# A new instruction order for a cross-attention and PReLU kernel, with a third buffer for its exponentials

## The chip, the cores and the metric

The kernel runs on one core of one Trainium2 chip. The metric is the device time of one execution in microseconds (us). The profile's *span*, from the first to the last instruction, is about 1.75 us shorter than that time. Engines: PE (TensorE, matmuls), ACT (ScalarE), DVE (VectorE), POOL (GpSimd), and SP, which here only issues DMAs. PSUM, where PE writes, has eight banks.

## What is computed

There are 8 batches, 8 heads, 512 tokens, 32 states, 64 features a head. Tokens attend to states, states attend to tokens, both results are put behind each other as 544 rows a batch of 512 features, and these go through a two-layer network with a PReLU.

```python
scores = scale * np.matmul(x, state.transpose(0, 1, 3, 2))
a = softmax(scores);   xread = np.matmul(a, state)        # 512 rows a batch
scores2 = scale * np.matmul(state, x.transpose(0, 1, 3, 2))
a2 = softmax(scores2); sread = np.matmul(a2, x)           # 32 rows a batch
x = concatenate([xread, sread], axis=2)                   # as rows of 8 * 64 features
h = x @ w_in                                              # 512 -> 2048
g = np.maximum(h, 0.0) + alpha * np.minimum(h, 0.0)
out = g @ w_out                                           # 2048 -> 512
```

## The kernel before

Since `xread @ w_in` is `a @ (state @ w_in)`, the kernel first makes the small state product m = state @ w_in, and the token weights a then meet m directly. All work is cut into steps, and the string `ORDER` (lines 17 to 102) lists them by hand, 1053 tokens. The loop at its end calls the steps in that order under a manual schedule, so each engine works through its own share of the list in exactly this order, and waits where an operand or a buffer isn't ready. A token names a step and its arguments; the last numbers of m, F, S, rd are PSUM banks k0 to k5, the last letter of mo, O, rdo the engine that copies (a is ACT, v is DVE). The steps that matter here, for batch b:

- `sc.b` (PE): both score products into the two-bank PSUM tile `two`, whose single buffer also serves some products m. It needs `xd.b`, a DMA that transposes x, issued by SP, which in turn needs `lx.b`, the load of x, issued by POOL.
- `tm.b`, `sb.b`, `smax.b` (DVE): the maximum over states, the scores' block transpose, the maximum over tokens. `te.b.g` (ACT): exponentials for the state reads, into the tile `e2`. `ssh`, `snorm` (POOL), `sexp` (ACT), `ssum`, `wb` (DVE): the rest of the token softmax, which ends in the weights aT.
- `tn.b.g` (POOL) scales `e2`; `tt.b` (SP) transposes it by DMA; `rd.b` (PE) are the state reads, `rdo.b` their copy.
- `m.b.f` (PE): a quarter f of the state product. Without banks in the token it goes to the two-bank tile (`m.0.3`, `m.1.3`, `m.6.0` and others), with banks (`m.5.1.2.0`) to two single ones. `mo.b.f.e.g` copies half g of it to SBUF on engine e. Its eight matmuls run in parallel on parts of the array, so one m takes about as long as one and a half matmuls of 512 columns.
- `F.b.jc.k` (PE): two matmuls of 512 columns, 128 hidden features of the batch, into bank k. `N.b.jc` (ACT): relu(-h) out of that bank, into one of four buffers. `G.b.jc` (DVE): the PReLU out of the same bank. After G the bank is free. `F.8.jc` is the same for all batches' state reads at once.
- `S.b.q.i` (PE): two matmuls of 512 columns, the part of hidden features 2i and 2i + 1 of the 128 tokens q; at i = 0 the token names the bank. After i = 7, `O.b.q.e` copies the bank out on engine e and SP writes it to memory (in two DMAs for batch 2, else in one), through four buffers in turn.

In the profile F is line 491 (`f`, its halves, line 512; of the reads line 500), S line 543, N line 523, G line 531, m line 458, mo line 480, sc line 308, rd line 433, O line 581, te line 400, tt line 418, xd line 275, tm line 389 and 392, sb line 341, smax line 349.

The excerpt of the list that the prediction speaks of (m.0.3, m.1.3 with their copies; the softmax of batch 1):

```
te.1.1 te.1.0 F.0.11.3 G.0.9 ssh.p.1 F.0.8.1 N.0.8 N.0.11 S.0.0.3 S.0.1.3 m.0.3 G.0.8 F.0.10.2
mo.0.3.a.0 N.0.10 sexp.1 S.0.2.3 mo.0.3.v.1 xd.2 G.0.11 G.0.10 S.0.3.0.1 m.1.3 S.0.3.1 mo.1.3.a.0
```

Of the kernel before, what the change touches and what calls it, by code (L numbers as in the profile page):

```python
# [38 lines left out]
S.1.1.3 ssum.2 F.1.14.0 F.1.15.2 snorm.p.2 mo.2.3.a.0 S.1.1.4 mo.2.3.a.1 S.1.1.5 m.3.2 m.4.2.1.4
N.1.14 tt.1 tsum.2 N.1.15 G.1.14 mo.3.2.a.1 S.1.1.6 S.1.2.3 S.1.2.4 mo.3.2.a.0 mo.4.2.a.0 G.1.15  # L40
mo.4.2.a.1 S.1.2.5 S.1.1.7 xd.3 O.1.1.a m.3.1.0.2 m.2.2.1.4 sc.3 wb.2 tn.2.1 S.1.2.6 S.1.2.7
mo.3.1.a.1 F.2.15.5 S.1.0.0.2 mo.2.2.a.0 mo.3.1.a.0 O.1.2.a lx.4 mo.2.2.a.1 sb.3 N.2.15 S.1.0.1 tm.3
F.2.13.1 N.2.13 G.2.15 S.1.0.2 F.2.4.0 tn.2.0 F.2.2.3 G.2.13 smax.3 N.2.4 F.2.9.4 F.2.0.5 N.2.9
S.1.0.3 S.1.0.4 G.2.9 S.1.0.5 N.2.2 N.2.0 te.3.0 F.2.12.1 S.1.0.6 N.2.12 G.2.2 G.2.4 G.2.0 xd.4
# [12 lines left out]
S.3.3.0.4 F.3.15.0 S.3.3.1 N.3.5 lx.6 G.3.5 te.5.0 te.5.1 N.3.10 N.3.15 S.2.2.3 F.3.12.5 S.2.2.4
N.3.11 S.3.3.2 lx.7 N.3.12 G.3.10 G.3.15 F.4.6.3 N.4.6 tn.4.0 F.4.5.0 G.3.11 F.4.3.1 N.4.5 S.2.2.5
G.3.12 G.4.5 S.3.3.3 F.4.4.5 S.3.3.4 F.4.7.0 N.4.4 S.3.3.5 S.2.2.6 N.4.3 sb.5 N.4.7 S.3.3.6 S.2.2.7
G.4.4 G.4.7 S.3.3.7 F.4.1.5 F.4.0.0 xd.6 O.2.2.a S.3.1.0.2 O.3.3.a S.3.1.1 F.4.9.4 N.4.1 smax.5  # L60
G.4.6 N.4.0 S.3.0.0.3 tn.4.1 S.3.0.1 G.4.1 G.4.0 F.4.8.5 S.3.1.2 tsum.5 N.4.9 ssh.p.5 G.4.3 sexp.5
N.4.8 G.4.9 F.4.11.0 F.4.2.1 N.4.2 S.3.0.2 ssum.5 S.3.0.3 S.3.0.4 tt.4 N.4.11 S.3.1.3 G.4.8 S.3.1.4
# [590 lines left out]
```

## Time and profile before

| | |
|---|---|
| time, median of 3 runs | 218.55 us (218.24 to 218.85) |
| the profiled execution | 218.35 us, its span 216.6 us |
| granted clock of TensorE | 1.00 throughout |
| matmuls | 1637, of them 746 of 512 columns in F (250) and S (496) |
| DMA | 23.12 MB, mean 107 GB/s |

A line of the profile's groups or of its timeline names the source line, the engine, the operation and what is written from what, with shapes; xN is the number of instructions taken together. In the timeline the first two numbers are start and length in us, and brackets hold the idle time of the engine before it and what ended that. Line 480, for instance, is every copy of a state product, whichever engine makes it. PE's busy time counts from a matmul's start to its modelled end, and matmuls overlap, so how full PE is shows better in the distance from one start to the next.

### The profile page before, as it was taken

What the parts mean: (1) busy time and instruction counts of PE and PEld (TensorE: products, weight loads), DVE (VectorE), ACT (ScalarE), POOL (GpSimd) and SP (SyncE); (2) the same over time, 40 slices, a digit from 0 to 9 for tenths busy, and PEclk for the clock granted to TensorE, in tenths of its full rate; (3) what the DMA queues carried; (4) which work ended last, traced back from release to release, by engine and by line L of the source; (5) the groups of instructions that cost most, each with busy time, mean ns of one, the idle gap of its engine ahead of it and who ended that gap; (6) DMA issues with size and microseconds to landing.
All of it is one profiled execution on the core that took longest, in us unless ns stands there. A gap on an engine that the chain in (4) does not pass through costs nothing.

```text
span 216.6 us, 4193 instructions
## 1 busy us (share of the span) xinstructions
PE 209.9 (97%) x1637; PEld 99.9 (46%) x1637; DVE 166.5 (77%) x253; ACT 137.2 (63%) x271; POOL 71.1 (33%) x58
## 2 busy tenths in 40 slices
PE   7889999999999999999999999999999999999994
PEld 2543334444444444544444445444454455554553
DVE  3699998899899999798998769977798466665001
ACT  3399984899987848786747937566545346544021
POOL 7383943730943703190337301802500000000000
PEclk9999999999999999999999999999999999999999
DMA  6999999496286694179652811041430011110124
GB/s 89 174 196 206 207 199 183 127 206 127 59 137 145 81 213 98 51 108 195 174 109 97 100 50 49 2 97 48 53 147 24 28 48 48 48 47 4 48 100 145
DMA packets 39716, 23.12 MB, mean 107 GB/s; under 512 B 22144, under 2 KB 35984, under 8 KB 39696
## 3 DMA queue, kind: packets, MB, share of 16 engines
q0 software_dynamic: 12704, 8.62, 28.2%
q1 hardware_dynamic: 26960, 14.23, 26.3%
q8 instruction: 13, 0.21, 0.5%
q14 instruction: 7, 0.06, 0.1%
q10 hardware_dynamic: 32, 0.01, 0.0%
HBM read 17.31 MB, written 8.91 MB: 121 GB/s over the span
## 4 chain that ended last, share of the span: by engine, by line
PE 90%; DMA 5%; POOL 2%; issue 1%; DVE 1%; ACT 0%; POOLq 0%
PE o L543 50%; PE h L491 25%; DMA w_in_sb<-in_moe_w_in_dram 5%; PE m_ps L458 4%; PE h L500 3%; PE o L591 3%; PE o L563 2%; PE sr_ps L433 2%; PE sc L308 1%; DVE m L480 1%; POOL xg L179 1%; POOL xg L162 0%; PE h L512 0%; POOL w_in_sb L198 0%; ACT m L480 0%
## 5 line engine op out<-in xcount | busy, mean ns | idle before, releaser
L543 PE MATMUL o<-w_out_sb,gt 128*128 128x512 f16 x496 | 125.3, 379 | 0.0
L523 ACT ACTIVATE neg<-h 128x512 f32<-128x512 f32 (+1 forms) x144 | 77.1, 579 | 46.8 <-PE h L491 37.4
L531 DVE SCALAR_TENSOR_TENSOR gt<-neg,oma_sb,h 128x512 f16<-128x512 f32 x128 | 89.9, 738 | 15.5 <-ACT neg L523 14.5
L543 PEld LDWEIGHTS <-gt 128*128 128x128 f16 x496 | 47.3, 98 | 55.3 <-issue 3.4
L491 PE MATMUL h<-aT,m 128*128 128x512 f16 x250 | 68.3, 379 | 0.0
L491 PEld LDWEIGHTS <-m 128*128 128x128 f16 x250 | 24.1, 98 | 28.3 <-issue 0.6
L414 POOL TENSOR_SCALAR e<-e,r 128x512 f16<-128x512 f16 x16 | 25.0, 1566 | 20.5 <-DVE r L410 16.6
L480 ACT CAST m<-m_ps 128x512 f16<-128x512 f32 x50 | 27.2, 611 | 4.5 <-PE m_ps L458 4.2
L369 POOL TENSOR_TENSOR an<-ts,r 128x1024 f16<-128x1024 f32 (+1 forms) x9 | 15.5, 1720 | 33.9 <-DVE r L366 14.8
L355 POOL TENSOR_TENSOR ts<-ts,mx 128x1024 f32<-128x1024 f32 (+1 forms) x9 | 15.5, 1721 | 28.7 <-DVE mx L349 28.7
L581 ACT COPY osb<-o 128x512 f32<-128x512 f32 x22 | 12.9, 591 | 14.9 <-PE o L543 14.9
L458 PE MATMUL m_ps<-w_in_sb,stT 64*32 64x512 f16 x256 | 11.4, 383 | 0.5 <-DMA w_in_sb<-in_moe_w_in_dram 0.4
L400 ACT ACTIVATE e<-sc,nb 128x512 f16<-128x512 f32 x16 | 11.2, 705 | 1.1 <-DVE nb L392 1.1
L377 DVE STREAM_TRANSPOSE aT<-an 128x1024 f16<-128x1024 f16 (+1 forms) x9 | 10.1, 1121 | 2.1 <-POOL an L369 2.1
L531 DVE SCALAR_TENSOR_TENSOR gs<-neg,oma_sb,h 128x256 f16<-128x256 f32 x16 | 7.5, 478 | 4.5 <-ACT neg L523 4.5
L480 DVE CAST m<-m_ps 128x512 f16<-128x512 f32 x14 | 9.1, 679 | 1.9 <-ACT m L480 1.6
L389 DVE TENSOR_REDUCE nb<-sc 128x2 f32<-128x1024 f32 x8 | 9.6, 1204 | 0.3 <-PE sc L308 0.3
L349 DVE TENSOR_REDUCE mx<-ts 128x32 f32<-128x1024 f32 (+1 forms) x9 | 9.8, 1091 | 0.0
L365 DVE TENSOR_REDUCE r<-ts 128x32 f32<-128x1024 f32 (+1 forms) x9 | 9.8, 1088 | 0.0
L500 PE MATMUL h<-XS,w_in_sb 128*128 128x256 f16 x64 | 9.4, 273 | 0.0
L601 DVE COPY osr<-o 128x512 f32<-128x512 f32 x1 | 0.7, 691 | 11.3 <-PE o L591 11.3
L361 ACT ACTIVATE ts<-ts 128x1024 f32<-128x1024 f32 (+1 forms) x9 | 8.7, 967 | 0.2 <-POOL ts L355 0.2
(52 smaller groups left out, 121.6 us busy)
## 6 DMA issues: line engine op xcount, KB each, us to landing
out_dram<-osb SPq DMA_DIRECT2D x27, 256.0 KB, 2.3
xg<-in_x_dram POOLq DMA_DIRECT2D x7, 512.0 KB, 7.0
w_in_sb<-in_moe_w_in_dram POOLq DMA_DIRECT2D x4, 512.0 KB, 8.7
w_out_sb<-in_moe_w_out_dram POOLq DMA_DIRECT2D x4, 512.0 KB, 7.9
out_dram<-osb SPq DMA_DIRECT2D x9, 128.0 KB, 2.1
xg<-in_x_dram POOLq DMA_DIRECT2D x2, 256.0 KB, 4.3
out_dram<-osr SPq DMA_DIRECT2D x2, 256.0 KB, 2.4
st<-in_state_dram POOLq DMA_DIRECT2D x1, 224.0 KB, 5.4
```

The lines of the kernel that those rows point to most:

```text
L355: engine(e).tensor_tensor(ts, ts, over_blocks(cols(live["mx", b], j, S // N)), ALU.subtract)
L369: engine(e).tensor_tensor(blocks(cols(live["an", b], j, S)), blocks(cols(live["ts", b], j, S)), over_blocks(cols(live["r1", b], j, S // N) ...
L400: nc.scalar.activation(live["e2", b][:, g, :, :], live["sc", b][:, :, :, g, :].rearrange("p r j s -> p (r j) s"), EXP, bias=live["nb", b][ ...
L414: nc.gpsimd.tensor_scalar_mul(e2, e2, live["r2", b][:, g : g + 1])
L458: nc.tensor.matmul(t[N * k : N * (k + 1), :], st_head(b, h)[64 * r : 64 * r + 64, :], w_in_sb[64 * r : 64 * r + 64, c, 512 * f : 512 * (f ...
L480: copier(e)(m_tile(b)[:, f, g, :], live["mp", b, f][g])
L491: nc.tensor.matmul(h.rearrange("p (r j s) -> p r j s", r=2, j=2), ms[b][:, f, g, 128 * j : 128 * (j + 1)], weights(b, g), start=(g == 0), ...
L500: nc.tensor.matmul(h, w_in_sb[:, c, 128 * jc : 128 * (jc + 1)], XS[:, c].rearrange("p q n b -> p (q n b)"), start=(c == 0), stop=(c == n_c ...
L523: nc.scalar.activation(neg, h, RELU, bias=0.0, scale=-1.0)
L531: nc.vector.scalar_tensor_tensor(gt, negs.pop((b, jc)), oma_sb[:, jc : jc + 1], h, ALU.mult, ALU.add)
L543: nc.tensor.matmul(outs[b, q], gts[b, jc][:, 128 * q : 128 * (q + 1)], w_out_sb[:, jc, :], start=(jc == 0), stop=(jc == n_jc - 1),)
L581: copier(e)(osb, t)
```

## The change

The list is rewritten from the second step of batch 0's third block of tokens (S.0.2.1) on. No step is added or taken away; the list has the same 1053 tokens. What differs is their order, the banks of most F, S, m and rd, and the engine of some copies. From F.5.11 on the order is the old one but for banks. The tile `e2` gets three buffers in place of two. The main lines:

```diff
-te.1.1 te.1.0 F.0.11.3 G.0.9 ssh.p.1 F.0.8.1 N.0.8 N.0.11 S.0.0.3 S.0.1.3 m.0.3 G.0.8 F.0.10.2
-mo.0.3.a.0 N.0.10 sexp.1 S.0.2.3 mo.0.3.v.1 xd.2 G.0.11 G.0.10 S.0.3.0.1 m.1.3 S.0.3.1 mo.1.3.a.0
...
-G.0.15 S.0.3.5 F.1.2.3 S.0.2.6 N.1.2 F.1.0.2 tsum.1 S.0.2.7 N.1.0 S.0.1.6 S.0.1.7 G.1.2 O.0.2.a sc.2
-m.2.1.3.4 S.0.0.6 O.0.1.a F.1.7.0 mo.2.1.a.0 mo.2.1.a.1 G.1.0 F.1.1.2 tm.2 sb.2 F.1.3.3 N.1.7
...
+te.1.1 G.0.6 smax.1 F.0.11.1 S.0.0.3 te.1.0 G.0.9 N.0.8 m.0.3 N.0.11 F.0.10.2 mo.0.3.a.0 S.0.1.3
+G.0.8 G.0.11 N.0.10 S.0.2.3 mo.0.3.a.1 ssh.p.1 S.0.3.0.3 G.0.10 m.1.3 sexp.1 m.2.1.1.2 S.0.0.4
+mo.2.1.a.1 S.0.2.4 mo.2.1.a.0 F.0.14.2 F.0.13.1 ssum.1 N.0.14 S.0.1.4 snorm.p.1 S.0.2.5 G.0.14
...
+S.0.3.3 G.0.12 S.0.3.4 F.1.2.1 G.0.15 N.1.2 S.0.1.6 mo.1.3.a.0 tn.1.0 G.1.2 S.0.2.6 S.0.1.7 sc.2
+tt.0 m.4.2.2.1 S.0.2.7 O.0.1.a F.1.3.0 mo.4.2.a.1 F.1.0.1 mo.4.2.a.0 F.1.1.2 O.0.2.a S.0.0.6 tm.2
...
-S.2.1.4 tn.3.1 N.3.1 N.3.9 G.3.1 S.2.1.5 S.2.0.2 G.3.4 tn.3.0 N.3.14 tm.4 F.3.3.5 F.3.8.1 G.3.14
-N.3.8 G.3.9 S.2.1.6 S.2.1.7 S.2.0.3 S.2.3.0.4 N.3.3 xd.5 O.2.1.a tt.3 sb.4 G.3.8 smax.4 F.3.6.2
...
-O.2.0.v m.5.1.2.0 mo.6.0.a.1 mo.5.1.a.1 rd.3.1 mo.6.0.v.0 rdo.3.a mo.5.1.v.0 rd.2.5 m.4.1.3.0 ssum.4
-sc.5 m.4.3.2.1 rdo.2.a S.2.3.6 mo.4.1.a.1 mo.4.1.a.0 tm.5 tsum.4 snorm.p.4 F.3.5.5 mo.4.3.a.0
...
+tn.3.0 O.2.1.a G.3.13 S.2.0.3 F.3.6.1 S.2.3.0.5 te.4.0 ssh.p.4 N.3.14 G.3.14 sexp.4 tsum.4 tn.4.1
+N.3.6 G.3.4 S.2.0.4 F.3.8.0 tt.3 N.3.8 S.2.0.5 S.2.3.1 S.2.0.6 S.2.3.2 F.3.3.2 F.3.9.3 ssum.4
+snorm.p.4 S.2.3.3 S.2.0.7 N.3.3 xd.5 S.2.3.4 G.3.8 N.3.9 G.3.3 S.2.3.5 m.6.0 G.3.6 G.3.9 m.5.1.0.2
+rd.3.1 rd.2.3 O.2.0.a mo.6.0.v.1 mo.5.1.a.0 m.4.1.4.0 mo.5.1.a.1 mo.6.0.v.0 sc.5 rdo.3.a m.4.3.2.1
...
             live["e2", b] = att.tile(
-                [128, 2, n_q, 128], F16, name=f"e2_{b}", tag="e2", bufs=2
+                [128, 2, n_q, 128], F16, name=f"e2_{b}", tag="e2", bufs=3
             )
```

The transposing DMAs and writes that SP issues stand in these orders (old, then new) from xd.2 to the last write of batch 2:

```
xd.2 tt.0 O.0.2 O.0.1 O.0.0 O.0.3 tt.1 xd.3 O.1.1 O.1.2 xd.4 O.1.0 O.1.3 tt.2 xd.5 O.2.1 tt.3 O.2.0 O.2.3 xd.6 O.2.2
xd.2 tt.0 O.0.1 O.0.2 O.0.0 O.0.3 tt.1 xd.3 xd.4 O.1.1 O.1.2 O.1.0 tt.2 O.1.3 O.2.1 tt.3 xd.5 O.2.0 O.2.3 O.2.2 xd.6
```

More of the change, by code (lines that the diff above doesn't have):

```diff
@@ L39 @@
[L39 to L44, printed above, removed]
@@ L57 @@
[L57 to L62, printed above, removed]
@@ new lines @@
+F.1.6.4 S.1.2.0.0 F.1.8.5 G.1.9 tt.1 m.2.3 S.1.2.1 N.1.6 N.1.8 G.1.4 F.1.12.3 G.1.6 F.1.11.2 ssh.p.2
+F.1.10.1 S.1.2.2 F.1.15.4 G.1.8 N.1.12 N.1.11 mo.2.3.a.0 S.1.1.0.5 S.1.1.1 N.1.10 S.1.2.3 G.1.12
+G.1.11 G.1.10 sexp.2 xd.3 F.1.13.3 N.1.15 S.1.1.2 N.1.13 ssum.2 F.1.14.2 N.1.14 mo.2.3.a.1 S.1.1.3
+G.1.13 G.1.14 S.1.2.4 S.1.1.4 S.1.1.5 G.1.15 m.3.2 mo.3.2.a.0 mo.3.2.a.1 m.3.1.1.3 rd.0.2 rd.1.4
+sc.3 snorm.p.2 lx.4 rdo.0.a mo.3.1.v.0 wb.2 rdo.1.a m.2.2.1.2 mo.3.1.v.1 S.1.1.6 xd.4 S.1.2.5
+S.1.2.6 F.2.4.4 S.1.1.7 F.2.2.3 mo.2.2.a.1 sb.3 S.1.2.7 S.1.0.0.2 tm.3 mo.2.2.a.0 N.2.4 F.2.15.1
@@ new lines @@
+O.1.1.a S.1.0.1 smax.3 S.1.0.2 F.2.0.5 O.1.2.v F.2.9.0 N.2.15 S.1.0.3 G.2.15 ssh.p.3 S.1.0.4 S.1.0.5
+N.2.0 N.2.9 tn.2.1 sexp.3 S.1.3.0.1 G.2.0 F.2.13.5 G.2.4 G.2.9 S.1.0.6 te.3.1 ssum.3 N.2.2 N.2.13
+G.2.13 F.2.12.4 F.2.8.0 N.2.12 N.2.8 S.1.3.1 S.1.3.2 G.2.12 S.1.3.3 te.3.0 G.2.2 F.2.1.5 S.1.0.7
+F.2.5.4 N.2.1 F.2.3.3 G.2.8 S.1.3.4 snorm.p.3 F.2.11.0 tn.2.0 G.2.1 O.1.0.a N.2.5 S.1.3.5 N.2.11
+tsum.3 S.1.3.6 N.2.3 G.2.5 m.3.3.2.5 sc.4 wb.3 F.2.6.4 tt.2 G.2.11 mo.3.3.a.1 mo.3.3.a.0 S.1.3.7
+S.2.1.0.5 G.2.3 F.3.1.2 N.2.6 F.3.13.0 O.1.3.a F.2.10.3 N.3.1 G.2.6 tm.4 F.2.7.1 N.3.13 N.2.7 N.2.10
@@ new lines @@
+mo.4.1.a.1 S.2.3.6 F.3.11.0 rdo.2.a mo.4.3.a.0 wb.4 N.3.11 mo.4.1.a.0 S.2.2.0.3 F.3.0.2 mo.4.3.v.1
+F.3.10.1 S.2.3.7 tm.5 S.2.2.1 S.2.2.2 G.3.11 N.3.0 F.4.1.4 sb.5 F.3.5.0 S.2.2.3 N.3.10 N.4.1 O.2.3.a
+N.3.5 S.2.2.4 G.3.10 G.3.0 F.3.7.1 F.4.11.5 F.4.7.2 lx.6 G.4.1 N.4.11 N.3.7 S.2.2.5 S.2.2.6 smax.5
+te.5.0 N.4.7 S.3.3.0.4 lx.7 S.2.2.7 G.3.5 ssh.p.5 S.3.3.1 O.2.2.a te.5.1 S.3.3.2 G.4.7 F.4.5.0
+F.3.15.3 N.4.5 G.3.7 N.3.15 G.4.11 tn.4.0 F.4.4.2 G.4.5 S.3.1.0.1 F.3.12.5 S.3.3.3 N.4.4 G.3.15
+G.4.4 N.3.12 G.3.12 sexp.5 F.4.6.0 N.4.6 S.3.3.4 ssum.5 F.4.8.3 S.3.1.1 F.4.3.2 S.3.1.2 F.4.0.5
@@ new lines @@
+S.3.3.5 S.3.3.6 N.4.3 S.3.3.7 N.4.8 G.4.6 N.4.0 S.3.1.3 S.3.1.4 xd.6 S.3.1.5 G.4.8 F.4.9.0 G.4.3
+F.4.2.3 G.4.0 S.3.0.0.2 N.4.9 S.3.0.1 S.3.0.2 N.4.2 tsum.5 O.3.3.v S.3.1.6 G.4.9 S.3.0.3 sc.6 G.4.2
+m.5.3.5.4 m.5.0.0.3 tm.6 snorm.p.5 S.3.0.4 S.3.0.5 mo.5.0.a.0 S.3.1.7 mo.5.0.a.1 mo.5.3.v.0 sb.6
+mo.5.3.a.1 F.4.10.0 S.3.2.0.3 N.4.10 F.4.14.5 S.3.2.1 S.3.2.2 S.3.2.3 wb.5 N.4.14 S.3.0.6 tt.4
+S.3.0.7 tn.5.1 F.5.3.4 O.3.1.a G.4.14 te.6.1 te.6.0 S.3.2.4 G.4.10 O.3.0.a m.7.2.1.5 m.5.2.0.2
+tn.5.0 mo.7.2.a.1 m.6.3 mo.5.2.v.0 S.3.2.5 mo.5.2.a.1 F.4.15.5 mo.6.3.a.1 mo.7.2.v.0 S.3.2.6
@@ new lines @@
+F.5.13.0 F.4.13.2 N.5.3 S.3.2.7 F.4.12.1 G.5.3 mo.6.3.a.0 N.4.15 S.4.0.0.4 S.4.0.1 G.4.15 S.4.0.2
+m.7.0 O.3.2.a N.4.13 N.5.13 xd.7 G.4.13 m.6.1.3.5 F.5.12.2 G.5.13 mo.6.1.a.1 F.5.15.0 S.4.0.3
+mo.6.1.a.0 N.5.12 smax.6 mo.7.0.v.0 N.5.15 F.5.1.5 G.5.15 S.4.1.0.3 S.4.1.1 S.4.1.2 N.5.1 F.5.2.0
+N.4.12 S.4.1.3 N.5.2 S.4.1.4 G.4.12 S.4.0.4 S.4.1.5 S.4.1.6 F.5.10.1 mo.7.0.a.1 S.4.0.5 ssh.p.6
+G.5.1 sexp.6 G.5.2 F.5.0.5 F.5.5.0 N.5.0 S.4.1.7 S.4.0.6 N.5.10 S.4.0.7 G.5.12 G.5.0 tt.5 S.4.2.0.2
+G.5.10 O.4.1.a N.5.5 rd.4.5 O.4.0.v rd.5.3 m.7.3.1.4 G.5.5 rdo.4.a m.6.2.5.0 rdo.5.a mo.6.2.a.0
@@ new lines @@
+S.6.0.2 N.8.10 O.5.3.v G.8.4 S.6.1.0.1 F.7.0.5 S.6.0.3 F.7.7.0 N.7.0 S.6.1.1 G.6.11 S.6.0.4 N.7.7
+S.6.0.5 G.7.0 S.6.1.2 F.8.14.4 S.6.1.3 S.6.1.4 G.8.10 S.6.0.6 N.8.14 F.7.3.5 S.6.0.7 G.7.7 S.6.1.5
+F.8.3.2 F.7.6.0 G.8.14 N.7.3 F.8.2.4 O.6.0.v G.7.3 F.7.2.3 F.8.9.5 S.6.1.6 N.8.3 G.8.3 S.6.2.0.2
+N.8.2 N.7.2 S.6.2.1 G.8.2 S.6.2.2 N.7.6 S.6.1.7 F.7.14.4 G.7.6 F.7.10.0 G.7.2 S.6.2.3 N.8.9 N.7.14
+G.7.14 O.6.1.a G.8.9 N.7.10 S.6.2.4 S.6.2.5 F.8.15.3 F.8.8.1 N.8.8 S.6.2.6 F.7.5.4 F.8.0.5 G.7.10
+N.8.15 S.6.3.0.0 N.8.0 G.8.15 N.7.5 S.6.2.7 G.8.0 F.8.12.3 G.7.5 S.6.3.1 S.6.3.2 F.8.11.5 F.7.1.4
@@ new lines @@
+G.8.8 N.8.12 F.7.15.1 O.6.2.a N.7.1 S.6.3.3 F.8.5.2 S.6.3.4 N.7.15 S.6.3.5 N.8.5 G.7.1 F.8.6.4
+N.8.11 G.8.12 S.7.2.0.3 G.7.15 F.7.4.1 G.8.11 N.8.6 F.8.1.5 G.8.5 S.6.3.6 N.8.1 N.7.4 F.8.7.2 G.8.6
+S.7.2.1 S.7.0.0.4 G.8.1 N.8.7 G.7.4 F.7.11.5 G.8.7 F.8.13.1 S.6.3.7 N.8.13 R.0.0.2 R.0.1 G.8.13
+R.0.2 O.6.3.v F.7.9.1 F.7.12.0 N.7.11 N.7.12 R.0.3 G.7.11 R.0.4 N.7.9 G.7.9 F.7.8.5 R.0.5 N.7.8
+S.7.2.2 S.7.2.3 R.0.6 F.7.13.1 G.7.8 S.7.0.1 G.7.12 S.7.0.2 R.0.7 S.7.0.3 S.7.0.4 N.7.13 RO.0.a
+S.7.1.0.5 R.1.0.0 S.7.2.4 S.7.1.1 S.7.1.2 S.7.1.3 L.7.3.1.0.2 S.7.1.4 R.1.1 S.7.2.5 R.1.2 G.7.13
```

76 lines of the change are left out of this document (22 added, 54 removed).

## The prediction

> **What bounds the kernel now.** I read the page first, then the chain of waits, the table of who waits for whom, the timeline of TensorE (PE) alone around the places that these name, and last the transposing DMAs. The page, and the chain in order of time (start, length, what):
>
> ```profile
> span 216.6 us, 4193 instructions
> PE 209.9 (97%) x1637; PEld 99.9 (46%) x1637; DVE 166.5 (77%) x253; ACT 137.2 (63%) x271; POOL 71.1 (33%) x58
> PE 90%; DMA 5%; POOL 2%; issue 1%; DVE 1%; ACT 0%; POOLq 0%
> ```
>
> ```profile
> 87.41 0.59 ACT m L480
> 88.03 1.30 DVE m L480 x2
> ...
> 107.27 3.02 PE o L543 x14
> ```
>
> PE is on the chain nine tenths of the time. Fourteen matmuls of 512 columns take 3.02 us, 0.216 each, so a step of two (an S or an F of a batch) takes 0.43, and that step is the floor. What can still be gained is where PE stands still. In the stretch that the change touches, from S.0.2.1 (24.3 us) to F.5.11 (134.8), I looked for matmuls that start later than the one before them allows. PE alone shows all of them:
>
> ```profile
> 27.78 1.03 PE L543 MATMUL o<-w_out_sb,gt 128*128 128x512 f16 x4
> 28.73 0.41 PE L458 MATMUL m_ps<-w_in_sb,stT 64*32 64x512 f16 x8
> 29.07 0.61 PE L491 MATMUL h<-aT,m 128*128 128x512 f16 x2
> 29.52 1.03 PE L543 MATMUL o<-w_out_sb,gt 128*128 128x512 f16 x4
> 30.58 0.41 PE L458 MATMUL m_ps<-w_in_sb,stT 64*32 64x512 f16 x8
> ```
>
> ```profile
> 88.83 0.40 PE L308 MATMUL sc<-xT,stT 64*32 64x256 f16 x16
> 89.37 0.41 PE L458 MATMUL m_ps<-w_in_sb,stT 64*32 64x512 f16 x8
> ```
>
> ```profile
> 93.18 1.11 PE L543 MATMUL o<-w_out_sb,gt 128*128 128x512 f16 x4
> 94.12 0.59 PE L491 MATMUL h<-aT,m 128*128 128x512 f16 x2
> 94.55 1.03 PE L543 MATMUL o<-w_out_sb,gt 128*128 128x512 f16 x4
> 95.46 0.59 PE L491 MATMUL h<-aT,m 128*128 128x512 f16 x2
> ```
>
> Four matmuls and the switch to a state product take 28.73 - 27.78 = 0.95 for m.0.3, but 30.58 - 29.52 = 1.06 for m.1.3: a stall of 0.11. From the scores sc.5 to m.4.3 pass 0.54, where sc.2 to m.2.1 took 0.23 (40.09 to 40.32, below): 0.31. Four matmuls with 1.11 in place of 1.03: 0.08. After 94.55 four steps should end at 95.41, the next starts at 95.46: 0.05. Together 0.55 us. I found no other in this stretch.
>
> The two large ones have one cause, seen with all engines in the timeline, and summed in the table of waits (total, times, longest):
>
> ```profile
> 29.21 0.59 ACT L480 CAST m<-m_ps 128x512 f16<-128x512 f32 x1
> 29.72 0.60 ACT L523 ACTIVATE neg<-h 128x512 f32<-128x512 f32 x1
> 29.83 0.69 DVE L480 CAST m<-m_ps 128x512 f16<-128x512 f32 x1 [0.42 <-ACT m L480]
> 30.21 1.05 ACT L361 ACTIVATE ts<-ts 128x1024 f32<-128x1024 f32 x1
> 30.44 1.40 DVE L531 SCALAR_TENSOR_TENSOR gt<-neg,oma_sb,h 128x512 f16<-128x512 f32 x2
> ```
>
> ```profile
> 86.93 0.62 PE L458 MATMUL m_ps<-w_in_sb,stT 64*32 64x512 f16 x16
> 87.41 1.07 ACT L480 CAST m<-m_ps 128x512 f16<-128x512 f32 x2 [0.99 <-PE m_ps L458]
> 88.03 1.29 DVE L480 CAST m<-m_ps 128x512 f16<-128x512 f32 x2 [1.16 <-ACT m L480]
> ```
>
> ```profile
> DVE m L480 <- ACT m L480: 1.6, 2, 1.2
> ```
>
> m.0.3 and m.6.0 are products in the two-bank tile, whose halves go to ACT and to VectorE (DVE). DVE's copy starts 0.03 after ACT's ends both times (29.80 to 29.83, 88.00 to 88.03): the second half waits for the first. m.1.3 then waits for 29.83 + 0.69 = 30.52 and starts at 30.58; m.4.3 waits for DVE's second copy, of m.5.1, at 89.32, and starts at 89.37. Between a copy's end and the matmul pass some 0.06.
>
> **What the change does to PE's own work.** Up to S.0.2.1, and from F.5.11 on, the order is the old one apart from bank numbers, which are renamed so that each bank's reuse keeps its distance. Between the two, both orders hold the same 226 two-matmul steps and the same 34 small groups (m, sc, rd). Only their runs differ: the old order breaks the stream of steps 12 times for small groups, the new one 11. A lone product costs 0.95 - 0.86 = 0.09 on entry and 29.07 - 28.73 = 0.34 itself; beside another small group it costs about 0.22. One break less is about -0.2; orders of pairs inside the runs give some back, and I take -0.15.
>
> **The copies.** mo.0.3 now goes wholly to ACT and mo.6.0 wholly to DVE, m.5.1's halves both to ACT. For m.0.3: ACT copies from 28.77 (m.0.3 now starts one step, 0.43, earlier), N.0.10 comes between as in the row at 29.72, the second copy ends by about 30.35, and m.1.3 is due at 30.47: no stall, -0.11. For m.6.0, now due at 86.93 - 0.11 - 0.43 (one step fewer ahead) - 0.2 = 86.2: two DVE copies start 0.48 later, as from 86.93 to 87.41, and take 1.29, to about 88.05 with the PReLU before them; sc.5, in the same bank pair, is due at 88.83 - 0.74 = 88.09, so 0.02 late. m.5.1's copies on ACT end at 86.4 + 0.48 + 1.07 = 87.95, well ahead of m.4.3 at 88.3. So -0.31 + 0.02. The places of the 0.08 and 0.05 no longer exist in the new order: -0.13. Each copy that changes engine costs 0.59 on ACT or 0.69 on DVE; there are 50 and 14 of them before and after, so no engine's load changes.
>
> The Trainium skill, "PSUM — Partial Sum Buffer", Specifications (TRN2), has ScalarE and VectorE reading PSUM in parallel at full bandwidth as long as they do not collide in a bank. By that rule the split of two halves over two banks costs nothing, and the -0.42 would not come from undoing it. The trace disagrees in this program: DVE sat idle 0.42 and 1.16 until ACT's copy was over, whatever the banks could do.
>
> **The third buffer for exponentials.** I cost it at nothing. With two, te.2 needs the transpose of batch 0's exponentials over. The views of the transposed tiles (forms, first and last start; then issue to landing):
>
> ```profile
> L418 SPq DMA_TRANSPOSE e2T<-e x8: 1237/1287/1457, 35.8 to 153.1; - x8
> DMA to landing us min/median/max: 3.1/3.6/4.7
> ```
>
> ```profile
> L275 SPq DMA_TRANSPOSE xT<-xg x6: 1682/2276/3011, 32.8 to 107.5; - x6
> DMA to landing us min/median/max: 4.2/4.3/5.1
> ```
>
> That lands by 35.8 + 4.7 = 40.5, and the scores that te.2 reads come no sooner than 38.9, with 1.5 us of maximum behind them. Without this cover it would still be ACT waiting, not PE.
>
> **What is moved, and how close it comes.** Two steps come much earlier. sc.2:
>
> ```profile
> 40.09 0.41 PE L308 MATMUL sc<-xT,stT 64*32 64x256 f16 x16
> 40.32 0.40 PE L458 MATMUL m_ps<-w_in_sb,stT 64*32 64x512 f16 x8
> 40.57 1.23 DVE L389 TENSOR_REDUCE nb<-sc 128x2 f32<-128x1024 f32 x1 [0.29 <-PE sc L308]
> ```
>
> It has three steps fewer ahead of it, m.2.1 more and the stall less: 40.09 - 1.30 + 0.22 - 0.11 = 38.90. Its transposed x, issued at 32.8, lands by 37.9: 1.0 to spare.
>
> m.2.1 goes from 40.3 to right behind m.1.3, 30.69, in the densest part of ACT and DVE. Its second bank is freed by G.0.10. F.0.10 now starts at 28.64, one step before the row's 29.07; its matmuls end 0.61 later; N.0.10 (0.60) follows after 0.04 and G.0.10 (0.74) after 0.04, to 30.67, and 0.06 to PE: 30.73, late by 0.04. Its two ACT copies stand behind the softmax's exponential (30.21 + 1.05), take 1.07, and free F.0.13's bank at 32.31, when F.0.13 is due (30.69 + 0.34 + 3 steps = 32.32). Neither is worth a tenth, but neither has room. I walked the new order so from bank to bank; some twenty places up to F.5.11 come out within 0.1 of their due time, none later than 0.05. For what they cost together the trace has no row. Below: 0, since a late place moves all behind it and gives those room. Above: 0.55, what the old order lost in the same stretch. I take 0.2, nearer the two unexplained losses of 0.08 and 0.05.
>
> **Queues passed.** The row on SP (the issuing queue) changes most: xd.4 now stands ahead of O.1.1, O.1.2 and O.1.0, whose four output buffers are not wanted again before batch 2, so that costs nothing. xd.5, the transpose for sc.5, falls behind both halves of O.2.1 and behind tt.3:
>
> ```profile
> 77.12 1.91 SPq L275 DMA_TRANSPOSE xT<-xg  x1
> 81.28 0.81 SPq L584 DMA_DIRECT2D out_dram<-osb  x2
> 82.20 1.24 SPq L418 DMA_TRANSPOSE e2T<-e  x1
> ```
>
> S.2.1.7 has two steps and a break fewer ahead of it, so O.2.1 is issued near 81.28 - 0.86 - 0.2 - 0.11 = 80.1, tt.3 near 80.95, xd.5 near 82.25, 5.1 later than before. It lands 4.2 to 5.1 later, 86.5 to 87.4; sc.5 is due at 88.09. It had 7 us to spare and has 0.7 to 1.6.
>
> **The sum.** -0.11 - 0.31 - 0.13 - 0.15 + 0.2 = -0.5. The profiled execution took 218.35 (span 216.6 and 1.75 around it), so 217.85; the median of the runs is 218.55, 0.2 above it, and I forecast 218.05 for a median of that kind, written as 218.0. From the bounds of the handoffs (0 and 0.55) this case runs from 217.85 to 218.4.
>
> **Rivals.**
> - Clean: the handoffs hold, or the old runs' other 0.2 was stall too. -0.7, 217.85. For it: the worked places are late by hundredths. Against it: so many without room.
> - DVE falls behind after sc.2. Sixteen steps and more now wait on banks that DVE frees behind sc.2's maximum and transpose.
>
> ```profile
> 45.00:50.00 5.00, 5.00 (x60) 2.43 (x59) 5.00 (x8) 4.49 (x10) 1.91 (x1) 1.00 1.25 230
> L531 DVE SCALAR_TENSOR_TENSOR gt<-neg,oma_sb,h 128x512 f16<-128x512 f32 x128 | 89.9, 738 | 15.5 <-ACT neg L523 14.5
> ```
>
>   DVE (third busy column, 5.00 of 5.00) has no idle there. From 39.4 to the end of G.1.8 stand the two scans and the transpose of sc.2 with the later maximum (3.7) and nine PReLUs at 0.66 when they overlap, as two in 1.40 show: 49.1, and S.1.1.0 is due at 49.4 (22 steps and two runs after sc.2). At their full 0.738 it is 0.4 late: 218.45. Against it: they overlapped throughout the old order.
> - The split was not the cause, as the skill's rule would have it: -0.13 - 0.15 + 0.2, about 218.45.
> - Slower: xd.5 comes late. If the transposing DMA does not start on x before tt.3 has landed (80.95 + 3.1 to 4.7), x lands 4.2 to 5.1 after that, 88.3 to 90.7, and PE waits at sc.5 with all behind it, 0.2 to 2.7, the middle 1.5: 219.55. It decides from 1.2 late on. Against it: xd.2 and tt.0 were also issued back to back (32.8, 35.8) and no x took over 5.1.
>
> **How the numbers follow.** A measurement here can tell about 0.3% from no change, 0.66 us: below 217.9 is faster, above 219.2 slower. Forecast 0.42 (0.11 of it faster, 0.31 within); clean 0.20 (0.17, 0.03); DVE behind 0.15 (0.13 within, 0.02 slower); split not the cause 0.05 (0.04 within, 0.01 slower); xd.5 late, 0.18 (0.01 within, 0.17 slower), which I leave that high because the spare time is so much less than it was. So faster 0.28, within 0.52, slower 0.20. The range runs from 217.6, the clean case with the runs' own scatter, to 219.3, which leaves out most of the late xd.5.
>
> **What would show it.** Right: the wait of DVE's m for ACT's m gone from the table; m.1.3 and m.4.3 at regular distance; PE's steps at 0.216 with F.5.11 near 134.3. Wrong: a gap of PE at sc.5 ended by xT (late xd.5); PE waiting at F or S steps between 39 and 51 for DVE's gt (DVE behind); stalls at the two products with both halves on one engine (split not the cause); or a PE that gains more than 0.73, which by this sum it has not to give.

## The result, and the profile after

| | before | after |
|---|---|---|
| median of the runs | 218.53 us (218.09 to 218.96, 22 runs) | 218.12 us (22 runs, lowest 217.47) |
| ratio after to before | | 0.9976, 95% interval 0.9969 to 0.9984 |
| the profiled execution | 218.35 us, span 216.6 | 218.09 us, span 216.3 |
| S.0.2.1 starts | 24.31 us | 24.72 us |
| F.5.11 starts | 134.84 us | 134.59 us |
| the stretch between | 110.52 us | 109.87 us |
| from F.5.11 to the last step, L.7.3.2.7 | 78.45 us | 78.45 us |

One execution of the changed kernel took 1221.65 us; the ratio leaves it out. The change gains 0.24% by this ratio, some 0.5 us as forecast (0.41 by the two medians). All line numbers are one lower in the changed kernel. Its page: the span, the engines' busy time, and the chain of waits by engine.

```profile
span 216.3 us, 4190 instructions
PE 208.6 (96%) x1637; PEld 99.3 (46%) x1637; DVE 164.8 (76%) x253; ACT 137.6 (64%) x271; POOL 71.1 (33%) x58
PE 90%; DMA 5%; POOL 2%; issue 1%; ACT 0%; POOLq 0%
```

PE is on the chain as before; DVE's 1% has gone from it. The timeline of all engines around the first two products, and around m.6.0:

```profile
28.71 0.41 PE L457 MATMUL m_ps<-w_in_sb,stT 64*32 64x512 f16 x8
29.19 0.59 ACT L479 CAST m<-m_ps 128x512 f16<-128x512 f32 x1
29.49 1.46 PE L542 MATMUL o<-w_out_sb,gt 128*128 128x512 f16 x6
29.69 0.60 ACT L522 ACTIVATE neg<-h 128x512 f32<-128x512 f32 x1
30.19 0.58 ACT L479 CAST m<-m_ps 128x512 f16<-128x512 f32 x1
30.88 0.64 PE L457 MATMUL m_ps<-w_in_sb,stT 64*32 64x512 f16 x16
31.45 1.04 PE L542 MATMUL o<-w_out_sb,gt 128*128 128x512 f16 x4
...
86.67 0.63 PE L457 MATMUL m_ps<-w_in_sb,stT 64*32 64x512 f16 x16
87.23 1.28 DVE L479 CAST m<-m_ps 128x512 f16<-128x512 f32 x2
87.34 1.07 ACT L479 CAST m<-m_ps 128x512 f16<-128x512 f32 x2 [0.83 <-PE m_ps L457]
88.30 0.48 ACT L443 CAST XS<-sr_ps 128x128 f16<-128x128 f32 x1
88.57 0.40 PE L307 MATMUL sc<-xT,stT 64*32 64x256 f16 x16
88.79 0.43 PE L457 MATMUL m_ps<-w_in_sb,stT 64*32 64x512 f16 x8
89.49 0.70 ACT L479 CAST m<-m_ps 128x512 f16<-128x512 f32 x1
89.59 0.65 DVE L479 CAST m<-m_ps 128x512 f16<-128x512 f32 x1
```

Six matmuls and the switch take 30.88 - 29.49 = 1.39, that is 0.96 and one step of 0.43: m.1.3 is no longer late. m.4.3 follows sc.5 by 0.22, where it took 0.54. The table of waits has no row of DVE's m for ACT's m any more. The last two rows are the halves of m.4.3, which sits in two single banks: there ACT and DVE copy at the same time. One wait of the same kind is left, the other way round, at m.1.1 in the start-up that both kernels share (0.2 before); m.1.1 too is a two-bank product split over both engines:

```profile
ACT m L479 <- DVE m L479: 0.3, 1, 0.3
```

The trace also records which semaphore each instruction waits for. DVE's copies at 29.83 and 88.03 in the kernel before wait for the one that ACT's instructions raise; its copies out of single banks (88.64 before, 89.59 after) wait for the one that PE raises. So the order of the two halves of a two-bank product is written into the program. These halves are parts of one tile, where single banks are two tiles; that this is the reason is likely, but no run tries it. The new kernel itself splits one more two-bank product, m.7.0, whose second copy (125.95) comes so long after the first (123.18) that it has nothing to wait for.

The start-up was 0.41 longer in this execution, in steps that both kernels share. Its first long piece on the chain of waits is one load, 11.44 us in the profile of before and 11.84 in that of after (first the old row, then the new):

```profile
5.68 11.44 DMA w_in_sb<-in_moe_w_in_dram
```

```profile
5.69 11.84 DMA w_in_sb<-in_moe_w_in_dram
```

Over the ten profiles in which this part is unchanged S.0.2.1 starts between 24.11 and 24.72, whichever kernel runs. The tail is 78.45 in all of them, although one step of POOL in it, tn.6.1, was moved too. So the stretch between is the sharp measure of an order, and the whole time carries half a microsecond of scatter from loads.

The transposes on SP (the row of xd.5, and of all six the time to landing):

```profile
82.74 2.17 SPq L274 DMA_TRANSPOSE xT<-xg  x1
```

```profile
DMA to landing us min/median/max: 4.3/4.5/4.8
```

xd.5 lands at 87.25, sc.5 starts at 88.57: 1.3 us to spare. Ahead of it tt.3 was issued at 81.39 and landed at 84.7. Had x waited for that, it would have landed at 88.9 or later; it took 4.5, the median of all six.

### The profile page after: what moved, and what is told of

Its sections match the earlier page's. It is cut to its first block, busy times and chain, and to the rows that moved or that the text cites. A ratio compares the mean times of both kernels' runs of the same rounds, so it can differ in the third digit from the quotient of the medians.

```text
span 216.3 us, 4190 instructions
## 1 busy us (share of the span) xinstructions
PE 208.6 (96%) x1637; PEld 99.3 (46%) x1637; DVE 164.8 (76%) x253; ACT 137.6 (64%) x271; POOL 71.1 (33%) x58
## 4 chain that ended last, share of the span: by engine, by line
PE 90%; DMA 5%; POOL 2%; issue 1%; ACT 0%; POOLq 0%
PE o L542 50%; PE h L490 25%; DMA w_in_sb<-in_moe_w_in_dram 5%; PE m_ps L457 4%; PE h L499 3%; PE o L590 3%; PE sr_ps L432 2%; PE o L562 2%; PE sc L307 1%; POOL xg L178 1%; POOL xg L161 0%; PE h L511 0%; POOL w_in_sb L197 0%; POOL st L191 0%; POOL ident masks.py:199 0%
## 5 line engine op out<-in xcount | busy, mean ns | idle before, releaser
L580 ACT COPY osb<-o 128x512 f32<-128x512 f32 x23 | 13.7, 595 | 14.7 <-PE o L542 14.6
L479 DVE CAST m<-m_ps 128x512 f16<-128x512 f32 x15 | 9.9, 677 | 1.4 <-PE m_ps L457 1.3
```

Source lines behind the costliest of these rows:

```text
L479: copier(e)(m_tile(b)[:, f, g, :], live["mp", b, f][g])
L580: copier(e)(osb, t)
```

## The experiments

**The copies alone**, in the order of before:

```diff
-mo.0.3.a.0 N.0.10 sexp.1 S.0.2.3 mo.0.3.v.1 xd.2
+mo.0.3.a.0 mo.0.3.a.1 N.0.10 sexp.1 S.0.2.3 xd.2
-O.2.0.v m.5.1.2.0 mo.6.0.a.1 mo.5.1.a.1 rd.3.1 mo.6.0.v.0 rdo.3.a mo.5.1.v.0
+O.2.0.v m.5.1.2.0 mo.6.0.v.1 mo.5.1.a.1 rd.3.1 mo.6.0.v.0 mo.5.1.a.0 rdo.3.a
```

> The order of before, with the two split products alone put right: both halves of m.0.3 are copied by ACT, both of m.6.0 by DVE, and both of m.5.1 by ACT. Nothing else moves, and the exponentials keep two buffers. Theory (one engine's copy of a half of the two-bank product waits until the other engine's copy of the other half is over): the row of DVE's m waiting for ACT's m is gone; m.1.3 starts 0.95 after the first matmul of the four ahead of it instead of 1.06 (0.11 gained); m.4.3 starts 0.2 to 0.35 after sc.5 instead of 0.54 (0.2 to 0.3 gained). The stretch from S.0.2.1 to F.5.11, 110.53 us before, becomes 110.1 to 110.25, and the time falls by 0.3 to 0.4 us, ratio 0.998 to 0.999. Rival (the split is not the cause; the two places were late for want of ACT or DVE time, and the new order of steps made the difference): the stretch stays at 110.45 to 110.6, ratio 1.000.

Ratio 0.9988 (0.9977 to 0.9998), stretch 110.10, so 0.42 of the 0.65. Its timeline at the two places:

```profile
29.53 1.03 PE L543 MATMUL o<-w_out_sb,gt 128*128 128x512 f16 x4
30.48 0.41 PE L458 MATMUL m_ps<-w_in_sb,stT 64*32 64x512 f16 x8
...
87.40 1.29 DVE L480 CAST m<-m_ps 128x512 f16<-128x512 f32 x2 [0.54 <-PE m_ps L458]
87.62 1.07 ACT L480 CAST m<-m_ps 128x512 f16<-128x512 f32 x2 [1.21 <-PE m_ps L458]
88.82 0.40 PE L308 MATMUL sc<-xT,stT 64*32 64x256 f16 x16
89.04 0.46 PE L458 MATMUL m_ps<-w_in_sb,stT 64*32 64x512 f16 x8
```

m.1.3 comes 0.95 after the four matmuls ahead of it (1.06 before), m.4.3 0.22 after sc.5 (0.54 before). At m.6.0 each engine has two copies, as before; only the split of one product over both has gone, and DVE starts at 87.40 instead of 88.03. So the split caused this stall. The two small losses at 93.7 and 95.5 are gone too, and two new ones have come, 0.09 ahead of F.1.2 at 37.4 and 0.06 behind m.4.3: a late place moves when what lies ahead of it is put right.

**The split put back** into the order of after:

```diff
-S.0.2.3 mo.0.3.a.1 ssh.p.1
+S.0.2.3 mo.0.3.v.1 ssh.p.1
-O.2.0.a mo.6.0.v.1 mo.5.1.a.0
+O.2.0.a mo.6.0.a.1 mo.5.1.a.0
```

> The order of after, with the second half of m.0.3 back on DVE and the first half of m.6.0 back on ACT, in the same places of the list. Theory (a split two-bank product is copied one half after the other): DVE's copy of m.0.3 starts 0.03 after ACT's ends and keeps DVE from G.0.10, so m.2.1, which needs that bank, is 0.3 to 0.5 late; at m.6.0 one engine again waits for the other and m.4.3 comes 0.1 to 0.4 late. The stretch from S.0.2.1 to F.5.11, 109.87 us in the profile of after, becomes 110.3 to 110.7; time 0.4 to 0.8 us above after's, so ratio to before 0.999 to 1.002. Rival (both engines copy at once and a half costs the same on either): both copies overlap in the trace, the stretch stays within 0.1 of 109.87, ratio 0.997 to 0.998 like after's.

Ratio 1.0005 (0.9996 to 1.0015), stretch 110.64: the whole gain is lost again, and more than the copies alone had brought. The timeline:

```profile
28.08 2.05 DVE L530 SCALAR_TENSOR_TENSOR gt<-neg,oma_sb,h 128x512 f16<-128x512 f32 x3
30.05 0.68 DVE L479 CAST m<-m_ps 128x512 f16<-128x512 f32 x1
30.65 0.74 DVE L530 SCALAR_TENSOR_TENSOR gt<-neg,oma_sb,h 128x512 f16<-128x512 f32 x1
30.79 1.05 PE L457 MATMUL m_ps<-w_in_sb,stT 64*32 64x512 f16 x16
...
87.47 1.56 ACT L479 CAST m<-m_ps 128x512 f16<-128x512 f32 x3 [0.65 <-PE m_ps L457]
88.08 0.69 DVE L479 CAST m<-m_ps 128x512 f16<-128x512 f32 x1 [0.45 <-ACT m L479]
88.90 0.48 ACT L443 CAST XS<-sr_ps 128x128 f16<-128x128 f32 x1
89.10 0.72 PE L457 MATMUL m_ps<-w_in_sb,stT 64*32 64x512 f16 x8
```

The sizes are as expected (the second half of m.2.1 comes 0.42 later than in after, that of m.4.3 0.30, m.1.3 0.06), the reasons only in part. At m.0.3 nothing waits for ACT: DVE is busy with its PReLUs until 30.1, and its copy then pushes G.0.10 to 30.65, whose bank m.2.1 needs (the x16 row lasts 1.05 instead of 0.64). At m.6.0 DVE does wait for ACT's copy, 0.45, but m.4.3 is late because ACT now has three copies ahead of the read's copy, which ends at 89.38. So here the split costs what it puts on the engine that has no room.

**Two buffers for the exponentials** in the order of after (`bufs=3` back to `bufs=2`):

> The order of after, with two buffers for the exponentials instead of three. Theory (the third buffer is worth nothing in this order): the first exponential of batch 2, which starts at 42.9 us in after, finds the transpose of batch 0's exponentials, issued at 37.1 to 38.4 and landed 3.1 to 4.4 later, over already; the closest later one is batch 4's at 75.2, behind the transpose of batch 2's issued at 69.8. So no exponential starts later, the stretch from S.0.2.1 to F.5.11 stays at 109.8 to 110.0, and the ratio to before is after's, 0.9976 within 0.001. Rival (the order needs the buffer): ACT waits at an exponential for a transpose, relus behind it come late, and matmuls with them: stretch over 110.1, ratio 0.999 or more.

Ratio 0.9979 (0.9956 to 1.0002, widened by one run of 220.26), stretch 109.87. The first exponential of batch 2 starts at 42.67, 18.19 behind S.0.2.1 as in after. The third buffer is worth nothing here.

**The transpose of batch 5's x issued too late**, xd.5 moved behind O.2.0:

```diff
-snorm.p.4 S.2.3.3 S.2.0.7 N.3.3 xd.5 S.2.3.4
+snorm.p.4 S.2.3.3 S.2.0.7 N.3.3 S.2.3.4
-rd.3.1 rd.2.3 O.2.0.a mo.6.0.v.1
+rd.3.1 rd.2.3 O.2.0.a xd.5 mo.6.0.v.1
```

> The order of after, with the issue of the transpose of batch 5's x put behind O.2.0's output on the issuing queue: 82.7 us becomes about 87. It prices the mishap that the prediction feared most. Theory (PE waits for this landing and has nothing else to do): x lands 4.2 to 5.1 after its issue, at 91.3 to 92.2, where sc.5 is due at 88.57; sc.5 waits 2.7 to 3.6, m.4.3 and all behind it as much, and the time grows by the same 2.7 to 3.6 over after's (ratio to before 1.010 to 1.014). Rival (the engines catch up: DVE and ACT work off what they owe during the wait, and later places where PE would have had to wait are gone): the stretch grows by under half of sc.5's wait, ratio under 1.006.

Ratio 1.0369 (1.034 to 1.0398), stretch 119.35: 9.5 us longer than after's, where the theory gave 2.7 to 3.6 and the rival less than half of the wait. A row of the chain of waits, two of PE's timeline, then a table by stretches of 2 us (length, busy time and instructions of PE, weight loads, DVE, ACT and POOL, granted clock, DMA share, GB/s):

```profile
87.38 8.70 DMA xT<-xg
```

```profile
31.41 1.02 PE L542 MATMUL o<-w_out_sb,gt 128*128 128x512 f16 x4 [0.41 <-DMA w_out_sb<-in_moe_w_out_dram]
96.12 0.63 PE L307 MATMUL sc<-xT,stT 64*32 64x256 f16 x16 [7.42 <-DMA xT<-xg]
```

```profile
90.00:92.00 2.00, 0.00 (x0) 0.00 (x0) 0.00 (x0) 0.00 (x0) 0.00 (x0) 1.00 0.88 196
...
94.00:96.00 2.00, 0.00 (x0) 0.00 (x0) 0.00 (x0) 0.00 (x0) 0.00 (x0) 0.50 1.39 181
...
98.00:100.00 2.00, 2.00 (x8) 0.79 (x7) 1.61 (x3) 0.96 (x2) 0.00 (x0) 0.71 0.06 8
```

The transpose took 8.70, not 4.5. sc.5 starts at 96.12 instead of about 88.5 (7.6); the clock of PE is at half from 92.35 to 99.18 by the trace's record, so 3.06 us of work ran at half speed, and from sc.5 to F.5.11 pass 1.4 more than in after; and a wait for w_out at 31.4, told below, makes the stretch 0.47 longer. Together 9.5, of which 9.0 are the price of the late transpose.

**The same with the loads of batches 6 and 7 out of the way.** In the run above these two loads of x (0.5 MB each) were issued by POOL at 88.2 to 90.0, as in after:

```diff
-F.4.7.2 lx.6 G.4.1 ... S.3.3.0.4 lx.7 S.2.2.7 G.3.5 ssh.p.5 S.3.3.1
+F.4.7.2 G.4.1 ... S.3.3.0.4 S.2.2.7 G.3.5 ssh.p.5 lx.6 lx.7 S.3.3.1
```

> The kernel with the late transpose of batch 5's x, and beside that the loads of batches 6 and 7 put behind the fifth batch's shift on their queue, so that they start near 96 in place of 88.2 us. Theory A (the transpose took 8.7 in place of 4.5 us because these loads, 0.5 MB each, ran on the same DMA engines, and PE's clock went to 0.5 only because the wait was so long): issued at 87.4, it lands at 91.6 to 92.5; sc.5, due at about 88.6, waits 3.0 to 3.9; the clock of the matmuls behind it is 0.9 or more; the stretch grows by 3 to 4.5 over after's 109.87, ratio to before 1.011 to 1.018. Theory B (the landing is late for another reason, such as O.2.0's output on the same queue just ahead of it): sc.5 still starts near 96, the matmuls behind it still run at half clock, and the ratio stays near 1.037.

Ratio 1.0312 (1.0281 to 1.0343), stretch 118.70. The chain, PE's timeline, and two of the stretches:

```profile
86.99 5.45 DMA xT<-xg
```

```profile
92.49 0.63 PE L307 MATMUL sc<-xT,stT 64*32 64x256 f16 x16 [4.18 <-DMA xT<-xg]
...
96.01 1.91 PE L490 MATMUL h<-aT,m 128*128 128x512 f16 x4
97.72 1.57 PE L542 MATMUL o<-w_out_sb,gt 128*128 128x512 f16 x6
...
117.94 0.41 PE L307 MATMUL sc<-xT,stT 64*32 64x256 f16 x16 [1.82 <-DMA xT<-xg]
```

```profile
90.00:92.00 2.00, 0.00 (x0) 0.00 (x0) 0.00 (x0) 0.00 (x0) 0.00 (x0) 0.78 0.89 197
94.00:96.00 2.00, 2.00 (x6) 0.64 (x5) 1.64 (x3) 0.77 (x3) 0.00 (x0) 0.50 0.00 0
```

Theory A holds for the landing (92.45, in its range): without the loads the transpose took 5.45, so 3.2 of the 8.7 were theirs. Where the other 1.0 over the usual 4.5 comes from was not tried; O.2.0's writes still stand just ahead of it on the queue. Theory A fell on the clock and on the time. A wait of 4.2 was enough to bring the clock to half, from 91.10 to 97.93 by the record; work resumed at 92.49, 4.4 behind its due time, so 5.4 us ran at half (four matmuls from 96.01 to 97.72, 0.43 each) and cost 2.7. And the loads started only at 104.2, where the expectation had them near 96, and made the next transpose late: sc.6 waits 1.8, which is the price of this experiment's own edit. 4.4 + 2.7 + 1.8 is the 8.8 of the stretch but for 0.1. The profiled execution was the slowest of four (224.35 to 226.50 us); by the ratios the two kernels with the late transpose lie 8.6 and 7.3 us above after.

**One more break** in the stream of steps, S.1.1.6 put between the reads and the scores:

```diff
-rd.1.4 sc.3 ... mo.3.1.v.1 S.1.1.6 xd.4
+rd.1.4 S.1.1.6 sc.3 ... mo.3.1.v.1 xd.4
```

> The order of after, with one step, S.1.1.6, put between the second state read rd.1 and the scores sc.3, so that the run of small groups there is cut in two: 12 breaks in the stretch in place of 11, and nothing else moves. Theory (one break costs what the prediction took, 0.2, read from 0.09 + 0.34 for a lone small group against 0.22 for one among others): the stretch from S.0.2.1 to F.5.11 grows from 109.87 to 110.0 to 110.1 (the stall of 0.03 at m.2.2 may go), ratio to before 0.998 to 0.999. Rival (breaks cost nothing, and what is left between the copies-only kernel at 110.10 and after at 109.87 is stalls alone, of which the copies-only kernel has 0.09 at 37.1 and 0.04 at 89.1): the stretch stays at 109.8 to 109.9, ratio 0.9975.

Ratio 0.9992 (0.9975 to 1.001), stretch 110.48, more than either theory. But most of it has nothing to do with the break; PE's timeline shows it far ahead of the edit:

```profile
30.58 0.64 PE L457 MATMUL m_ps<-w_in_sb,stT 64*32 64x512 f16 x16
31.72 1.02 PE L542 MATMUL o<-w_out_sb,gt 128*128 128x512 f16 x4 [0.50 <-DMA w_out_sb<-in_moe_w_out_dram]
```

S.0.0.4 waits for the third quarter of w_out. From m.2.1 to S.0.0.4 pass 0.92, in after 0.34; without these 0.57 the stretch would be 109.91. What is left of the break is 0.04: from rd.1 to S.1.2.5 pass 1.69 instead of 1.65. But this is a difference of two things, as m.2.2 and the steps behind it show, first in after, then here:

```profile
56.16 0.46 PE L457 MATMUL m_ps<-w_in_sb,stT 64*32 64x512 f16 x8
56.55 1.47 PE L542 MATMUL o<-w_out_sb,gt 128*128 128x512 f16 x6
```

```profile
56.95 0.40 PE L457 MATMUL m_ps<-w_in_sb,stT 64*32 64x512 f16 x8
57.29 1.04 PE L542 MATMUL o<-w_out_sb,gt 128*128 128x512 f16 x4
```

The step behind m.2.2 comes 0.39 after it in after and 0.34 here: a stall of 0.06 has gone, so the break itself costs 0.1. All of that is the way in, as a step ahead of a small group takes 0.53 instead of 0.43. On the way out, by the traces, a product or the scores take 0.33 when a step comes next and 0.22 when another small group does, but a read takes 0.59 before either. So a break behind products or scores costs 0.2 and one behind a read 0.1.

**The third quarter of w_out.** POOL loads w_out in four quarters of 0.5 MB (wo.0 to wo.3); the steps S.b.q.4 and S.b.q.5 read the third. Before, the first of them is S.0.2.4 at 31.79, 7.48 behind S.0.2.1; in after it is S.0.0.4 at 31.45, 6.73 behind. By the traces the quarter landed between 29.8 and 31.7. One kernel asks for it later, with eight steps permuted in their own places (the expectation speaks of ten), and after itself ran once more beside it:

```diff
-m.2.1.1.2 S.0.0.4 mo.2.1.a.1 S.0.2.4 ... S.0.1.4 ... S.0.2.5 ... S.0.1.5 ... S.0.0.5 ... S.0.3.1 S.0.3.2
+m.2.1.1.2 S.0.3.1 mo.2.1.a.1 S.0.3.2 ... S.0.0.4 ... S.0.2.4 ... S.0.1.4 ... S.0.2.5 ... S.0.1.5 S.0.0.5
```

> The order of after, with ten steps of batch 0 permuted in their own places, so that the first step on the third quarter of w_out (S.0.0.4, at 31.4 us in after) stands where S.0.1.4 stood, 4 steps later, and S.0.3.1 and S.0.3.2 go ahead of it. No other engine's order changes. Theory (after asks for that quarter 6.73 us behind S.0.2.1 where before asked 7.48 behind it; the load lands at 29.8 to 31.7 in the profiles so far; so after waits for it in some executions, as the late-transpose and the more-break kernels did by 0.41 and 0.50, and that is what is missing between the 0.65 of the stretch and the 0.4 to 0.5 of the medians): no wait of PE for w_out in the profile, the stretch from S.0.2.1 to F.5.11 at 109.8 to 109.9 whatever the load does, and the median 0.1 to 0.2 below after's, ratio to before 0.9965 to 0.997. Rival (the missing part is start-up that scatters alike in all kernels, and the load's wait is rare): median within 0.05 of after's, ratio 0.9975 to 0.998.

> The kernel after itself once more, beside the one with the third quarter of w_out asked for later, so that both share a chip and the runs of before. Theory: ratio to before 0.997 to 0.9985 as measured, 0.0005 to 0.001 above its neighbour's; the stretch is 109.85 to 109.9 if w_out lands by 6.7 us behind S.0.2.1, and longer by just as much as it lands later. Rival: the two kernels agree within 0.0003.

Asked for later 0.9971 (0.9956 to 0.9985), after again 0.9974 (0.996 to 0.9988); the medians even stand the other way, 218.06 and 217.78. Both stretches are 109.87, as w_out landed at 30.17 and 30.04, in time for either. So the expected 0.1 to 0.2 did not show: the wait is too rare or too small for 7 and 12 runs that scatter by 0.9 and 1.4. The load was therefore pushed back in both kernels:

```diff
-m.1.2.2.3 wo.2 tn.0.0
+m.1.2.2.3 tn.0.0 wo.2
```

> The order of after, with the load of w_out's third quarter issued behind the scaling tn.0.0 on its queue in place of ahead of it: about 1.55 us later, near 25.3 in place of 23.3 to 23.8 us. Theory (after has 0 to 1 us of spare time for this load and pays 1:1 beyond it): the quarter lands at 31.4 to 33.0, S.0.0.4 waits 0.3 to 1.6 us for it, the stretch from S.0.2.1 to F.5.11 is 110.2 to 111.5 instead of 109.87, and the median is 0.3 to 1.5 above that of the kernel that asks for the quarter later. Rival (the queue's work in this place has time enough, the load lands when it always did because memory, not its issue, sets it): stretch 109.87, median like after's, ratio 0.9975.

> The same later load, in the kernel that asks for the third quarter of w_out four steps later (S.0.0.4 at 33.07 in place of 31.45 us). Theory: with 1.6 us more of spare time the later load is covered, wholly or but for 0.1 to 0.3 us; the stretch is 109.87 to 110.1 and the ratio to before 0.997 to 0.998. Rival (as for the kernel beside it): the two are alike.

In the order of after 1.0018 (1.0003 to 1.0033) and a stretch of 110.69; asked for later, 0.9987 (0.9971 to 1.0003) and 109.88. The first one's chain of waits:

```profile
25.13 6.88 DMA w_out_sb<-in_moe_w_out_dram
32.01 0.04 issue
32.05 1.02 PE o L542 x4
```

The load lands at 32.01, 0.8 behind S.0.0.4's due time, and the stretch is 0.82 longer; by the ratios the two kernels are 0.7 us apart. In the six profiles with after's order there, the load landed between 1.2 ahead of its due time and 0.5 behind it. So after has about a microsecond of spare time for this load at best and pays 1:1 beyond it, and four steps of delay cover it.

## Why the prediction was right, and where it was not

- *The bound, and the split as the cause of the two large stalls*: right. The copies alone took 0.42 off the stretch and both stalls went: -0.10 at m.1.3 for -0.11, -0.32 at m.4.3 for -0.31.
- *The rule of the Trainium skill's "PSUM — Partial Sum Buffer", Specifications (TRN2)*, by which a split would cost nothing: the prediction has the trace disagree with it, and that reading was wrong. For the two-bank tile the trace shows the wait again (0.45 at 88.08 in the kernel with the split put back), but it is a wait for ACT's semaphore, so whether the two banks could be read at once no run shows. Out of two single banks both engines copy at once (89.49 and 89.59), and over all the traces ACT's copies that overlap one of DVE's take 0.59 in the median, as the others do; there the trace agrees with the rule.
- *The two small losses*, -0.13: gone in after. They also went with the copies alone, so a place that is late by hundredths does not belong to an order as I treated it; others came elsewhere.
- *One break less*, -0.15: the stretch's -0.65 less -0.10, -0.32 and the -0.12 of the small losses, and less the 0.11 of new stalls (next item), leaves -0.22. So the price read from the rows (0.2) was right for a break between products, and what I took back for pairs inside the runs was not there. It is no fixed price, as the break at rd.1 cost 0.1.
- *Handoffs*, +0.2: mis-sized, and not the whole of it. Between engines the profile of after lost 0.11, half of what I took (0.06 behind m.2.2, 0.03 behind m.4.3, 0.02 behind m.2.1). What I did not weigh is a load: the new order asks for w_out's third quarter 0.75 earlier, and of the six profiles with this order at that place and nothing late ahead of it (after twice, two buffers, both late transposes, one more break) two waited and were 0.47 and 0.57 longer for it, or 0.17 on average over the six.
- *The sum*, -0.5: that it came out so near is luck in part. -0.10 - 0.32 - 0.12 - 0.22 + 0.11 is the stretch's -0.65, 0.15 more than I forecast, and a load that I had not weighed takes about as much back on average. It agrees with ratios of 0.9976 and 0.9974, which are 0.52 and 0.57 us; but the runs cannot tell this from scatter, as after and the kernel that asks later came out alike.
- *Small slips*: I had 50 copies of products on ACT and 14 on DVE in both kernels; after has 49 and 15, one copy more on DVE. And the "four steps" that should end at 95.41 are four matmuls, two steps. Neither changes the sum.
- *The third buffer at nothing*: right, 109.87 with two.
- *sc.2, m.2.1, xd.5*: counted from S.0.2.1 they came where they were put. sc.2 at 39.33, less the start-up's 0.41, is 38.92 (38.90 worked out); m.2.1 30.70 (30.73); xd.5's issue 82.33 (82.25); sc.5 88.16 (88.09); F.5.11 134.18 (134.3).
- *Rivals.* The stretch of after gains 0.65 of Clean's 0.7, but not because all handoffs held; the median, 218.12, lies nearer the forecast of 218.05 than Clean's 217.85. DVE did not fall behind: G.1.8 ends at 49.48 and S.1.1.0 starts on time at 49.85. That the split was not the cause fell with the copies alone. xd.5 was not late, and the mechanism I feared, that x's transpose starts only when tt.3 has landed, did not show: it landed 2.6 after tt.3, not 4.2 or more.
- *The price of a late xd.5* was the worst figure of the prediction. It made the cost equal to the delay ("0.2 to 2.7"); a start of sc.5 that was 7.6 late cost 9.0, and one 4.4 late cost 7.0, without the next late transpose. A delay as short as 0.2 to 2.7 was not run. The prediction left out that the same reads rd.3 and rd.2 that free the loads' buffers let 1 MB of loads start at 88.2, into the middle of a late transpose, and that PE's clock falls while PE waits.

## What to carry to other kernels

Where PE sets the time, first compare the distance from start to start with that of the same steps elsewhere; the two largest stalls here were 0.1 and 0.3 us, and both came from a product copied half by each engine. Where one engine's copy waits for another's, look which semaphore it waits for before blaming the memory. When an order is moved, work out the spare time of every load that the moved steps read, not only of the buffers that the engines hand each other: one load of weights had about 1 us to spare here, and stood in no row of the waits before. And price a late transfer by what starts beside it and by the clock after the wait, not by the wait alone.
